# Another order for four pairs of w2 rows in a state-space and dense layer

## The chip, the cores and the metric

The kernel runs on one core of one Trainium2 chip. The metric is device time in microseconds (us). The engines are TensorE (PE, with its weight loads as PEld), VectorE (DVE), ScalarE (ACT), GpSimd (POOL) and SyncE (SP), which here only issues transfers. SP, ACT and POOL each have a queue of transfers; all queues share the core's 16 DMA engines.

## The reference

The input x is 2048 tokens by 1024. After a layer norm (xn) the output is the sum of x, a diagonal complex state-space layer and a dense layer, in bfloat16:

```python
xn = _layernorm(x, axis=-1)
return x + _A_ref(xn, A_Lambda_re, ..., A_Dskip) + _B_ref(xn, B_w1, B_b1, B_w2)

# A: Bu = xn @ B_bar^T (complex); h_t = Lam_bar * h_(t-1) + Bu_t
#    y = 2 * real(h @ C^T) + xn * Dskip
# B: h = xn @ w1 + b1 (1024 -> 3584);  act = h * tanh(softplus(h))
#    act @ w2 (3584 -> 1024)
```

The activation is Mish. "Dense 1" below is xn @ w1, "dense 2" is act @ w2.

## The kernel before, in words

**Blocks.** The tokens are worked in four blocks of 512. Each block runs dense 1 with Mish, the input product of the state-space layer (B), a rotation, a scan along the tokens, the rotation back, and then dense 2 and the output projection (C), which add up in the same eight PSUM banks; DVE adds x and empties the banks (L1676), and the rows go out. The first block does all this plainly. The second does dense 2 plainly, but most of dense 1 and the B product by a scheme with seven products of halves in place of eight; the third and fourth use such a scheme for dense 2 too.

**Order.** The order of the work is written out by hand: one string of short names for each block (FIRST, WHOLE, STEPS, LAST), walked by `perform`. Each operation goes to its engine's list with the waits that its tiles call for; an engine works its list strictly in order. So a wait of an instruction holds all that stand behind it on that engine, and a transfer leaves when its queue's engine comes to it.

**The ring.** Weights stream through seven slots of 4 KB per partition (`ring`). SP issues one load each time that PE, and where told ACT, has done with a slot. The list `items` fixes what is loaded; for the first two blocks the dense 2 part of it is

```python
items += [("w2", g) for g in W2_ORDER]
```

A pair g is two tiles of 128 w2 rows, 2g and 2g + 1, of 28. `in_order(n, us)` runs tile 2 * W2_ORDER[n // 2] + n % 2 for the PSUM banks us, and the strings name n alone (`da20` is the n-th tile in order, not tile 20). A pair is 16 matmuls with 512 columns (L1544), whose stationary operand is a piece of the tile of `act` with the same number. `row_sizes` (first block) and `sizes_of` with `late_sizes` (second block, for the last four pairs) have ACT take the absolute row sums of the w2 rows in the slot (L1312, L1319) and follow the same table.

**What waits for act tiles.** When dense 2 has read an act tile, its memory takes something else. In the second block `m2` has POOL load raw w2 rows in two halves, the first into act tiles 20 to 23 and the second into tiles 24 to 27 (`d2_load`, L1264); `m3` loads two more halves into tiles 8 to 15. `h8` to `h11` scale the rows on ACT (L1279), POOL stores some of them to the DRAM buffer w2d (L1269), and four steps on DVE (`kd0`, L1297) turn them into the sums that the third block's dense 2 needs; each overwrites a half that must have been stored. Both halves of one load count on one semaphore. In the first block POOL loads rows of the B matrices into act tiles (`rows_load`, L1443), of which the fifth waits for tile 21 by an extra line; ACT takes their sizes (L1448).

**Around the end of the second block.** SP issues four DMA transposes of the next block's xn (`tr0` to `tr3`, L653) between the ring loads of C (`ring<-ctd`). PE's first products of the third block (L1063) write banks that DVE has to empty first, and some read units that DVE makes in place (L1238).

Of the kernel before, what the change touches and what calls it, by code (L numbers as in the profile page):

```python
# [142 lines left out]
def bass_parallel_sum__ssm_conv_s5__dense_activation_mish__prompt_kernel(  # L143
    nc: bass.Bass,
    A_x: bass.AP,
    A_Lambda_re: bass.AP,
    A_Lambda_im: bass.AP,
    A_B_re: bass.AP,
    A_B_im: bass.AP,
    A_C_re: bass.AP,  # L150
    A_C_im: bass.AP,
    A_log_dt: bass.AP,
    A_Dskip: bass.AP,
    B_x: bass.AP,
    B_w1: bass.AP,
    B_b1: bass.AP,
    B_w2: bass.AP,
    out: bass.AP,
):
    build_kernel(nc, A_x, A_Lambda_re, A_Lambda_im, A_B_re, A_B_im, A_C_re, A_C_im,  # L160
                 A_log_dt, A_Dskip, B_w1, B_b1, B_w2, out)


def build_kernel(nc, A_x, A_Lambda_re, A_Lambda_im, A_B_re, A_B_im, A_C_re, A_C_im,
# [19 lines left out]
    GROUPS = ((0, 7), (7, NPL), (NPL, NPL + 8), (NPL + 8, NF), (12, 16), (16, 20), (20, 24), (24, 28))  # L184
    TILES = [*range(12)]
    NFG = {2: 5, 3: GF}
    W2_ORDER = tuple(range(14))
    EARLY, LATE = ((0, 20),), ((20, 28),)
    PLAIN = [(f, f + 1) for f in (24, 10, 12, 26)]
    PASSING = {}  # L190
# [252 lines left out]
    for blk in range(NB):  # L443
# [7 lines left out]
        else:  # L451
            items += [("w2", g) for g in W2_ORDER]
        items += [("c", j) for j in range(NJ)] if blk >= FAST else []
# [853 lines left out]
    def row_sizes(g):  # L1307
        s = (NF // 2 + g) % NRING
        for j in range(2):
            r = 2 * W2_ORDER[g] + j  # L1310
            src = ring[:, s, j * D:(j + 1) * D]
# [3 lines left out]
    def late_sizes(g, s):  # L1315
        for j in range(2):
            r = 2 * W2_ORDER[g] + j
            src = ring[:, s, j * D:(j + 1) * D].rearrange("p (d t) -> p d t", d=2)
            aop(lambda e, src=src, r=r: e.activation(CT[:, 0:2, 1, TB:D], src, AF.Abs, accum_out=wp[:, r:r + 1]),  # L1319
                reads=[b_ring[s]], writes=[b_snap[0], b_wp])  # L1320
# [207 lines left out]
    def perform(blk):  # L1528
# [10 lines left out]
        for f0 in range(20, NF, 2) if blk == FAST else ():  # L1539
            left[at_item[blk, "w2", W2_ORDER[f0 // 2]]] += 1  # L1540

# [32 lines left out]
        def dense(f, us, chained=False):  # L1574
            g = (4 * REAL[f // 4] + f % 4) // 2 if split else f // 2
            at = at_item[blk, "w2", g]
            s = at % NRING
            assert n_item[0] <= at < n_loaded[0]
            wt = ring[:, s, :].rearrange("p (f d) -> p f d", f=2)
            for u in us:  # L1580
                q, h = u // 2, u % 2
                t, b_t = place(blk, f)
                opens = first[u]
                first[u] = False
                mm2(u, t[:, q * P:(q + 1) * P], wt[:, f % 2, h * TB:(h + 1) * TB], [b_t, b_ring[s]], at, opens=opens,
                    chained=chained, tell=f % 2 == 1 and u == us[-1])

        def in_order(n, us):
            dense(2 * W2_ORDER[n // 2] + n % 2, us)

        def sizes_of(g):
            at = at_item[blk, "w2", W2_ORDER[g]]
            late_sizes(g, at % NRING)
            if used(at):
                release()
# [279 lines left out]
```

## Time and profile before

| | |
|---|---|
| median of 3 runs | 591.37 us (590.75 to 593.43) |
| profiled execution, its own time | 591.81 us |
| its span | 590.6 us |
| PE busy in the span | 582.7 us |
| DVE, ACT, POOL busy | 511.2, 402.0, 151.9 us |
| first block's dense 2 on PE (L1544, act) | from 85.07, 48.51 us |
| second block's dense 2 on PE | from 228.97, with its last 218 matmuls from 232.01 |
| second block's output projection on PE | from 279.06, 27.79 us |
| transferred | 160.84 MB, mean 272 GB/s |

A row of a timeline gives start and length in us, engine, line and operation, output and inputs, and in brackets how long the engine was idle before and what ended that. DMA issues are counted from the issuing instruction to the landing of the data. The granted clock was 1.0 throughout.

### The profile page before, as it was taken

Reading aid. Unit: us, or ns where it says so; the run is one execution under the profiler, and the core shown is the slowest. Engines: PE = TensorE matmul, PEld = TensorE weight load, DVE = VectorE, ACT = ScalarE, POOL = GpSimd, SP = SyncE. Lnnn points to the kernel's source line nnn. Section 1 sums busy time; section 2 is a strip of 40 time slices with the busy share of each in tenths; the row PEclk is TensorE's granted clock in tenths of the full one; section 3 lists DMA queues with packets and bytes.
Section 4 is the critical chain, followed back from the end, with each engine's and each line's share of the span. In section 5 each row is a group of like instructions: output and inputs, shape, how many; then the busy total and the mean of one; then the engine's idle time right before and its main releaser. Section 6 shows DMA issues by size and latency. Waiting matters only on the chain.

```text
span 590.6 us, 9767 instructions
## 1 busy us (share of the span) xinstructions
PE 582.7 (99%) x3631; PEld 353.0 (60%) x3631; DVE 511.2 (87%) x784; ACT 402.0 (68%) x541; POOL 151.9 (26%) x215
## 2 busy tenths in 40 slices
PE   9999999999999999999999999999999999999998
PEld 8644444444447887444448888644446888854444
DVE  6999999999796878998957789999997569789995
ACT  4859995489297778999636779976222788892330
POOL 2899200134424421332161243200000013100000
DMA  9999999999668987999999959998945946989832
GB/s 242 309 243 263 231 179 221 316 326 361 226 243 279 322 291 262 338 309 207 273 396 394 348 205 299 333 335 252 290 157 196 388 184 214 339 320 317 296 118 72
DMA packets 115369, 160.84 MB, mean 272 GB/s; under 512 B 55802, under 2 KB 66682, under 8 KB 115322
## 3 DMA queue, kind: packets, MB, share of 16 engines
q1 hardware_dynamic: 98512, 107.31, 60.6%
q0 software_dynamic: 13728, 45.62, 22.4%
q10 hardware_dynamic: 3082, 7.29, 3.4%
q8 instruction: 29, 0.48, 0.3%
q14 instruction: 18, 0.15, 0.1%
HBM read 114.05 MB, written 34.08 MB: 251 GB/s over the span
## 4 chain that ended last, share of the span: by engine, by line
PE 88%; DMA 5%; DVE 3%; ACT 3%; issue 1%; POOL 0%; DVEq 0%
PE ps L1544 44%; PE ps L1063 15%; PE ps L985 11%; PE ps L1755 10%; PE ps L1773 5%; DMA act<-in_B_w_dram 2%; DMA w2d<-act 1%; PE ps L713 1%; DMA ring<-w2d 1%; PE ps L722 1%; DMA w2d<-hb 1%; DVE xx L1676 1%; ACT act L1279 1%; ACT hb L1279 1%; PE ps L675 1%
## 5 line engine op out<-in xcount | busy, mean ns | idle before, releaser
L1544 PE MATMUL ps<-ring,act 128*128 128x512 bf16 (+1 forms) x716 | 156.2, 379 | 0.0
L1544 PEld LDWEIGHTS ps<-ring,act 128*128 128x128 bf16 (+1 forms) x716 | 70.0, 98 | 83.3 <-DMA ring<-w2d 0.2
L1544 PE MATMUL ps<-ring,hT 128*128 128x512 bf16 (+1 forms) x390 | 83.4, 376 | 0.0
L1083 ACT ACTIVATE snaps<-ps,par,cs 128x256 f32<-128x256 f32 x100 | 54.5, 562 | 40.8 <-PE ps L1063 38.5
L947 DVE TENSOR_TENSOR mt<-hT,tab 128x2048 bf16<-128x2048 bf16 (+1 forms) x56 | 68.0, 1214 | 0.4
L1544 PEld LDWEIGHTS ps<-ring,hT 128*128 128x128 bf16 x390 | 38.1, 98 | 45.0
L1406 DVE TENSOR_TENSOR_SCAN hT<-cs,qi,hT 128x512 bf16<-128x512 f32 x48 | 60.1, 1273 | 0.0
L1063 PE MATMUL ps<-TT,ring 128*128 128x256 f16 x480 | 59.8, 273 | 0.0
L1755 PE MATMUL ps<-xnT,ring 128*128 128x512 bf16 x264 | 57.3, 379 | 0.0
L1100 DVE SCALAR_TENSOR_TENSOR act<-ps,cs,snaps 128x512 bf16<-128x512 f32 x54 | 39.4, 747 | 16.0 <-PE ps L1063 13.9
L1063 PE MATMUL ps<-xnT,ring 128*128 128x256 bf16 x400 | 50.4, 273 | 1.4 <-DVE xx L1676 1.4
L1063 PEld LDWEIGHTS ps<-TT,ring 128*128 128x128 f16 (+1 forms) x480 | 46.8, 98 | 6.5
L1269 POOL DMA_DIRECT2D w2d<-hb x35 | 25.0, 716 | 87.4 <-ACT hb L1279 50.4
L1755 PEld LDWEIGHTS ps<-xnT,ring 128*128 128x128 bf16 x264 | 25.8, 98 | 31.0
L1063 PEld LDWEIGHTS ps<-xnT,ring 128*128 128x128 bf16 (+1 forms) x400 | 38.9, 98 | 6.8 <-issue 1.9
L1650 ACT ACTIVATE hT<-hT,wz 128x1024 bf16<-128x1024 bf16 x16 | 18.0, 1146 | 36.5 <-DVE hT L1646 36.5
L931 ACT ACTIVATE act<-act 128x2048 bf16<-128x2048 bf16 (+3 forms) x13 | 33.0, 2559 | 2.0 <-DVE act L1086 1.9
L1010 DVE TENSOR_TENSOR hT<-ps,snaps 128x512 f16<-128x512 f32 x36 | 23.8, 687 | 11.9 <-ACT snaps L1002 10.0
L938 ACT ACTIVATE act<-act,cs 128x512 bf16<-128x512 bf16 x48 | 30.8, 708 | 0.1
L1212 POOL DMA_DIRECT2D wsd<-hb x35 | 19.0, 546 | 42.2 <-DVE hb L1238 25.4
L1766 ACT ACTIVATE act<-ps,par 128x512 bf16<-128x512 f32 (+1 forms) x40 | 23.6, 660 | 8.2 <-PE ps L1755 8.2
L1223 ACT ACTIVATE hb<-hb,cs 128x2048 bf16<-128x2048 bf16 x10 | 19.4, 1995 | 14.1 <-DVE xx L1676 12.7
(237 smaller groups left out, 1038.2 us busy)
## 6 DMA issues: line engine op xcount, KB each, us to landing
ring<-wsd SPq DMA_DIRECT2D x110, 256.0 KB, 4.9
ring<-in_B_w_dram SPq DMA_DIRECT2D x52, 512.0 KB, 5.5
ring<-ctd SPq DMA_DIRECT2D x24, 512.0 KB, 4.6
ring<-w2d SPq DMA_DIRECT2D x24, 512.0 KB, 4.7
ring<-w2d SPq DMA_DIRECT2D x36, 256.0 KB, 4.6
wsd<-hb POOLq DMA_DIRECT2D x35, 256.0 KB, 4.8
w2d<-hb POOLq DMA_DIRECT2D x35, 256.0 KB, 5.1
hb<-in_B_w_dram POOLq DMA_DIRECT2D x20, 256.0 KB, 5.4
```

Source lines behind the costliest of these rows:

```text
L931: aop(lambda e: e.activation(t, t, AF.Mish), reads=b, writes=b)
L938: aop(lambda e, a=a, y=y: e.activation(a, a, AF.Copy, scale=y), reads=[b_a, b_y], writes=[b_a])
L947: vop(lambda e: e.tensor_tensor(mt[:], u.unsqueeze(1).to_broadcast([P, 2, 2, TB]), tab[:, :, j, :].unsqueeze(2).to_broadcast([P, 2, 2, TB] ...
L985: PE.mm(lambda e, w=w, x=x, o=o, begin=begin, end=end: e.matmul(ps[:, bank, o:o + TH], lhsT=w, rhs=x, start=opens and begin, stop=end, ski ...
L1063: PE.mm(lambda e, w=w, x=x, o=o, begin=begin, end=end: e.matmul(ps[:, bank, o:o + TH], lhsT=w, rhs=x, start=opens and begin, stop=end, ski ...
L1083: aop(lambda e, o=o, p=p, j=j: e.activation(o, p, AF.Identity, scale=ig, bias=b1(f0 + j)), reads=[b_ps[b], b_par, b_ig], writes=b_dst)
L1100: vop(lambda e: e.scalar_tensor_tensor(out=dst, in0=bank(b), scalar=ig, in1=src, op0=ALU.mult, op1=ALU.add), reads=[b_ps[b], b_snap[k], b_ ...
L1269: PO.dma(lambda e: e.dma_start(w2d[at // 4][:, at % 4 * TB:(at % 4 + 2) * TB].rearrange("p (j t) -> p j t", j=2), t[:, :, d, :]), sem, rea ...
L1406: vop(lambda e: e.tensor_tensor_scan(out=hT[:, ci, j, :], data0=cj("r", j).to_broadcast([P, TB]), data1=hT[:, ci, j, :], initial=init, op0 ...
L1544: PE.mm(lambda e: e.matmul(ps[:, bank, lo:hi], lhsT=lhsT, rhs=rhs, start=opens, stop=last, skip_group_check=split), reads=reads, writes=[b ...
L1755: PE.mm(lambda e, k=k, w=w: e.matmul(ps[:, bank, :], lhsT=w, rhs=xnT[:, k, :], start=k == 0, stop=k == NK - 1), reads=[b_ring[s]] + b_xnT, ...
L1773: PE.mm(lambda e, ci=ci, k=k: e.matmul(ps[:, bank + ci, :], lhsT=BT[:, ci, j, k, :], rhs=xnT[:, k, :], start=k == 0, stop=k == NK - 1), re ...
```

## The change

One table is given another order:

```diff
-    W2_ORDER = tuple(range(14))
+    W2_ORDER = (*range(10), 12, 10, 11, 13)
```

Dense 2's last four pairs are loaded and multiplied in the order 12, 10, 11, 13, so the act tiles are read in the order 24, 25, 20, 21, 22, 23, 26, 27. The numbers of instructions and transfers are the same. The table serves the first and the second block; the third and fourth don't use it.

On PE, this is the second block's dense 2 near its end: a row with x15 ends a place (one pair of w2 rows); the names in brackets are what the matmul ahead of it waits for (d_ring1 to d_ring3: ring loads; q_ac: ACT). The changed row opens the last place but one; the row behind it belongs to the same place.

```order
 L1544 MATMUL ps<-ring,act 128x512 [waits d_ring1]
 L1544 MATMUL ps<-ring,act 128x512 x15
-L1544 MATMUL ps<-ring,act 128x512 [waits d_ring2,q_ac]
+L1544 MATMUL ps<-ring,act 128x512 [waits d_ring2]
 L1544 MATMUL ps<-ring,act 128x512 x15
 L1544 MATMUL ps<-ring,act 128x512 [waits d_ring3]
```

Tile 24, the first of the last group of four to get its Mish from ACT, was first read at the last place but one; now it is read two places earlier, where PE waits for ACT anyway, and its former place, which holds tiles 22 and 23 now, waits for the ring alone.

On POOL, this is the list around the second block's raw w2 loads; it reads the same in both kernels (q_pe: PE; L1212 stores units of w1, L1269 stores scaled w2 rows).

```order
L1212 DMA wsd<-act 128x1024 [waits q_ac]
L1212 DMA wsd<-act 128x1024
L1212 DMA wsd<-act 128x1024 [waits q_ac]
L1264 DMA act<-in_B_w_dram 128x2x1024 [waits q_pe] x2
L1264 DMA act<-in_B_w_dram 128x2x1024 x2
L1269 DMA w2d<-act 128x2x512 [waits q_ac] x2
L1269 DMA w2d<-act 128x2x512
```

The first of the two waiting loads needs tiles 20 to 23. The last matmul that reads them has moved from the third-last place to the last but one; the other load still needs tiles 26 and 27, read at the last place.

The third piece is POOL at the end of the first block, where w1 units are loaded into act tiles 24 to 27 and then 20 to 23 (L1137), behind the carry of the scan (L1419, L1421):

```order
 L1419 TENSOR_TENSOR qi<-qi,qt 128x8 [waits q_po]
 L1421 TENSOR_TENSOR qi<-qi,qt 128x8 [waits q_po]
-L1137 DMA act<-in_B_w1_dram 128x4x256 [waits q_pe] x2
+L1137 DMA act<-in_B_w1_dram 128x4x256
+L1137 DMA act<-in_B_w1_dram 128x4x256 [waits q_pe]
 L1137 DMA act<-in_B_w1_dram 128x4x256
 L1137 DMA act<-in_B_w1_dram 128x4x256 [waits d_nat4]
```

The load into tiles 24 and 25 no longer has a wait for PE of its own, since POOL waited for a later matmul before (tile 21, for L1443).

## The prediction

> **What bounds the kernel now.** I read the page's busy times first, then PE's own waits, then the chain of waits around the second block's end.
>
> ```profile
> PE 582.7 (99%) x3631; PEld 353.0 (60%) x3631; DVE 511.2 (87%) x784; ACT 402.0 (68%) x541; POOL 151.9 (26%) x215
> PE ps L1063 <- DVE xx L1676: 1.4, 1, 1.4
> PE ps L1063 <- DVE act L1238: 1.3, 1, 1.3
> ```
>
> TensorE (PE) is busy for 582.7 of 590.6 us, and no matmul goes away. What a new order can win lies in PE's waits (the columns are total us, times, longest). These two make 2.70 us together. The next rows, PE's timeline, place them at the seam between the second block's projection and the third block's first products.
>
> ```profile
> 232.01 47.22 PE L1544 MATMUL ps<-ring,act 128*128 128x512 bf16 x218
> 279.06 27.79 PE L1544 MATMUL ps<-ring,hT 128*128 128x512 bf16 x128
> 308.29 1.03 PE L1063 MATMUL ps<-xnT,ring 128*128 128x256 bf16 x8 [1.43 <-DVE xx L1676]
> 314.08 1.05 PE L1063 MATMUL ps<-TT,act 128*128 128x256 f16 x8 [1.27 <-DVE act L1238]
> ```
>
> The chain of waits (start, us, what) says why DVE is late there:
>
> ```profile
> 279.65 11.96 DMA act<-in_B_w_dram
> ...
> 291.63 4.28 ACT act L1279 x4
> ...
> 297.07 6.91 DMA w2d<-act
> ...
> 304.06 0.70 DVE act L1297
> ...
> 307.01 4.53 DVE xx L1676 x4
> ...
> 313.43 0.61 DVE act L1238
> ```
>
> Raw w2 rows come from DRAM into act tiles 20 to 27 in two halves. The half issued at 279.65 takes 11.96 us; only then can ACT scale the rows (L1279), POOL store them, and DVE overwrite them (L1297). DVE runs in order, so its L1676, which empties PSUM for PE, and its L1238 are late as well. From 304.06 to 314.04 DVE has no idle time worth naming, so this stretch moves as one piece.
>
> **What the change moves.** I count the pairs of dense 2 as places 0 to 13. From 232.01 to 279.06 PE runs 218 matmuls, 0.2158 us each; a place has 16, so 3.45 us. Place 13 starts at 275.6, place 12 at 272.15.
>
> ```profile
> 272.62 0.72 POOL L1264 DMA_DIRECT2D act<-in_B_w_dram  x1 [1.93 <-PE ps L1544]
> 279.65 2.14 POOL L1264 DMA_DIRECT2D act<-in_B_w_dram  x3 [6.32 <-PE ps L1544]
> ```
>
> The first half writes tiles 20 to 23. Before, their last reader stood at place 11 and the load followed at 272.62. With 12, 10, 11, 13 it stands at place 12, so the load is issued at 272.62 + 3.45 = 276.07. The second half needs tiles 26 and 27, still at place 13, and stays at 279.65 with the two loads behind it. On POOL nothing but these waits behind the moved load. ACT waits for both halves by one semaphore, so the 3.45 us cost nothing directly as long as the first half lands before the second: by its row below it landed at 283.1, the second at 291.6.
>
> What changes is the traffic that it meets. These rows, the DMA issues in narrow windows (one issue each; last number: us from issue to landing), are in order of issue, at 262.49, 265.92, 272.55, 272.62, 274.95 and 279.65:
>
> ```profile
> xnT<-xn SPq DMA_TRANSPOSE x1, 5.1
> xnT<-xn SPq DMA_TRANSPOSE x1, 4.3
> xnT<-xn SPq DMA_TRANSPOSE x1, 10.2
> act<-in_B_w_dram POOLq DMA_DIRECT2D x1, 512.0 KB, 10.5
> xnT<-xn SPq DMA_TRANSPOSE x1, 14.0
> act<-in_B_w_dram POOLq DMA_DIRECT2D x1, 512.0 KB, 12.0
> ```
>
> Between them SP issues loads of the C rows; one in the earlier, quieter stretch, at 262.05, and the two transposes at the raw loads read:
>
> ```profile
> ring<-ctd SPq DMA_DIRECT2D x1, 512.0 KB, 4.4
> 272.55 1.24 SPq L653 DMA_TRANSPOSE xnT<-xn  x1
> 274.95 1.59 SPq L653 DMA_TRANSPOSE xnT<-xn  x1
> ```
>
> Four equal transposes: the first two took 5.1 and 4.3 us, the third, issued 0.07 us before the first half, 10.2, and the fourth, into which the second half runs, 14.0. The table by stretches (last columns: DMA share, GB/s) shows what such a meeting does to all transfers:
>
> ```profile
> 268.00:270.00 2.00, 2.00 (x12) 0.88 (x10) 2.00 (x4) 2.00 (x2) 1.11 (x2) 1.00 1.14 293
> 276.00:278.00 2.00, 2.00 (x11) 0.89 (x10) 1.39 (x9) 1.91 (x4) 0.00 (x0) 1.00 1.09 114
> 286.00:288.00 2.00, 2.00 (x11) 0.94 (x10) 1.93 (x4) 0.91 (x1) 0.00 (x0) 1.00 0.27 77
> 288.00:290.00 2.00, 2.00 (x11) 0.89 (x10) 1.90 (x3) 0.00 (x0) 0.00 (x0) 1.00 1.03 393
> ```
>
> While a raw load and a transpose are in flight together the rate falls to 114 and 77 GB/s; alone, or after, it is 293 to 393. Now there are two such meetings, one after the other. With the first half issued at 276.07 the third transpose, at the 4.3 to 5.1 us of its predecessors, ends at 276.9 to 277.7, when the load has barely begun. One meeting, with the fourth, is left.
>
> How much earlier the second half lands (call it d) the trace of before doesn't show, so I bound it. From the good side: ACT's next free moment. From the bad side: the second half queues behind the first in POOL's queue and is pushed by the whole 3.45 us.
>
> ```profile
> 279.24 7.66 ACT L1223 ACTIVATE hb<-hb,cs 128x2048 bf16<-128x2048 bf16 x4
> 291.63 4.27 ACT L1279 ACTIVATE act<-act,cs 128x1024 bf16<-128x1024 bf16 x4 [4.72 <-DMA act<-in_B_w_dram]
> ```
>
> ACT idles 4.72 us, so d lies between -3.45 and 4.72. Between: if the first half meets the fourth transpose as it met the third, it lands at 276.07 + 10.5 = 286.6; the second half's 512 KB behind it, at half of 393 GB/s because SP's ring loads share the engines, take 2.7 us more: 289.3, so d = 2.3. If there is no real meeting any more, d reaches 4.72. I take 2.3 to 4.7, nearer the low end.
>
> PE gains as much as d until its own waits are gone: the projection ends at 306.85, and the 2.70 us are all there is. Below that DVE isn't the limit either: the last L1676 (4.53 / 4 = 1.13 us) can start at 306.85, which with the 2.5 us from its end (311.54) to that of L1238 (314.04) gives 310.5, before PE is there at 314.08 - 2.70 = 311.38. So the term is -2.3 to -2.7; I take -2.4.
>
> [...]
>
> **The other moved parts.** The new place 10 needs tile 24 earlier. ACT's last Mish of this block ends at 241.79, PE comes to place 10 at 265.2; no cost, with 23 us of cover.
>
> ```profile
> 234.49 7.30 ACT L931 ACTIVATE act<-act 128x2048 bf16<-128x2048 bf16 x4
> ```
>
> The table W2_ORDER also serves the first block, which the few words on the change don't say. There the loads of projection rows (L1443) wait for tile 21, which is now read a place later:
>
> ```profile
> 124.13 0.54 POOL L1443 DMA_DIRECT2D act<-in_A_B_re_dram  x1 [11.97 <-PE ps L1544]
> 131.04 1.06 ACT L1448 ACTIVATE act<-act 128x1024 bf16<-128x1024 bf16 x1 [0.23 <-DMA act<-in_A_B_re_dram]
> 135.90 1.28 DVE L866 SCALAR_TENSOR_TENSOR CT<-CT,cs,ct 128x1024 bf16<-128x1024 bf16 x1
> 158.66 2.36 DVE L1676 TENSOR_TENSOR xx<-ps,xx 128x1024 bf16<-128x1024 f32 x2 [3.15 <-PE ps L1544]
> ```
>
> So 124.13 becomes 127.58. ACT already waits 0.23 us for the third of these loads at 131.04; it will wait about 3.4 us more, and the scaling that DVE needs for its L866 at 135.90 shifts from an end near 133.2 to 136.6. I estimate 0.7 us of delay on DVE. It has 3.15 us of idle time before 158.66, so PE sees nothing; without that cover it would cost 0.7 us. POOL's later loads and ACT's scalings shift by up to 3.5 us, before ACT's long idle time. Ring loads are as many and as large as before; which w2 rows they fetch costs nothing.
>
> **The sum.** The profiled execution took 591.81 us (its span of 590.57 and 1.24 around it): 591.81 - 2.4 = 589.4. It lies 0.44 us above the median of 591.37, so the median becomes 589.0.
>
> **Rivals.**
>
> First, no change, 591.4 (590.9 to 591.9). The second half meets the fourth transpose whatever the first does, and it is the one on the chain. For it: its issue at 279.65 doesn't move, and the low rates last until 288. Against: it landed in a queue that had just spent 10 us on the first half and third transpose, which also held up the fourth.
>
> [...]
>
> Third, slower: the first half, now 3.45 us closer to the second, meets the fourth transpose and both loads pile up on it. From the moment that the second half lands after 291.61 every us costs PE one us, since DVE is full from 304 to 314. At the whole 3.45 us: 594.8; at half, 593.1. For it: POOL's queue holds the two in order, and the fourth transpose is the slowest already. Against: the third transpose and a ring load leave the engines earlier, and the data of both halves are no more than before.
>
> Fourth, the first block decides: the row loads slip by more than 3.45 us in the traffic of their time, and DVE's delay exceeds 3.15 us; each us above costs one. At a slip twice as large, with DVE delayed by 4.2 us, it takes back 1.0 us: with the gain 590.0, without it 592.4.
>
> **How the numbers follow.** Forecast 0.58, first and second rival together 0.22, the third 0.14, the fourth 0.06. The forecast's own range is 588.2 to 590.2: the 2.70 us and a few tenths of a median's scatter below, half of the gain above. For 8 in 10 I go over the unchanged case to 592.2, the weaker part of the third rival's. The bound of 0.5% (about what a measurement of this kernel can tell from no change) is 2.96 us. The two waits hold 2.70, so faster by over that needs the whole of them and some help from scatter or from later stretches: a third of the forecast, 0.20. Slower by over 0.5% needs 594.3, most of the pile-up and a little of the fourth: 0.11. The rest, 0.69, is within 0.5%.
>
> **What would show it.** The first half issued at about 276.1 (the step on the places); the third transpose landing in about 5 us instead of 10.2 (the meeting); the second half landing at 287 to 289.5 and ACT's L1279 starting then; DVE's L1297 starting before 302; PE's waits at the seam below 0.5 us together. It is wrong if the third transpose is fast and the second half lands no earlier, if DVE's L1676 starts at 307 or later, or if the idle time before 158.66 in the first block is gone.

## The result, and the profile after

| | before, same chip | changed |
|---|---|---|
| median of 11 executions | 593.25 us (590.29 to 596.26) | 588.03 us (587.57 to 591.76) |
| profiled execution, its own time | 591.81 us | 587.96 us |
| its span | 590.6 us | 586.7 us |

The ratio is 0.9927, with a 95% interval of 0.9901 to 0.9953: the changed kernel is 0.5 to 1.0% faster on this chip. The forecast was 589.0, with a range of its own from 588.2 to 590.2; 588.03 lies 0.17 us below that range, and the gain of 0.73% is nearly double the 0.4% forecast. The before column holds a second lesson: its eleven executions spread over 6 us, ten of the eleven changed ones over 0.75 us (587.57 to 588.32).

PE's waits of the changed kernel (total us, times, longest), the three largest:

```profile
PE ps L675 <- DVE filler L499: 1.0, 1, 1.0
PE ps L713 <- DMA ring<-in_B_w_dram: 0.7, 2, 0.5
PE ps L1544 <- DMA ring<-w2d: 0.7, 2, 0.5
```

Both waits of L1063, 1.4 and 1.3 us before, are gone. POOL's timeline and the DMA issues show where that comes from. The issues (KB, and last the us from issue to landing) stand in order of issue: four transposes at 262.78, 266.21, 272.84 and 275.24, then the raw halves at 276.37 and 279.94.

```profile
276.37 0.72 POOL L1264 DMA_DIRECT2D act<-in_B_w_dram  x1 [5.39 <-PE ps L1544]
279.94 2.14 POOL L1264 DMA_DIRECT2D act<-in_B_w_dram  x3 [2.86 <-PE ps L1544]
```

```profile
xnT<-xn SPq DMA_TRANSPOSE x1, 5.5
xnT<-xn SPq DMA_TRANSPOSE x1, 4.4
xnT<-xn SPq DMA_TRANSPOSE x1, 4.6
xnT<-xn SPq DMA_TRANSPOSE x1, 5.8
act<-in_B_w_dram POOLq DMA_DIRECT2D x1, 512.0 KB, 7.8
act<-in_B_w_dram POOLq DMA_DIRECT2D x1, 512.0 KB, 7.2
```

The whole execution runs 0.30 us later up to here (the projection starts at 279.36, before at 279.06). Less that, the first half leaves at 276.07, where the prediction had put it, and the second has not moved. The last two transposes take 4.6 and 5.8 us in place of 10.2 and 14.0, the second half 7.2 in place of 12.0. The table by stretches has the rates (last column, GB/s), 278 and 393 where 114 and 77 stood; over the eight stretches from 272 to 288 us the mean is 291 in place of 154:

```profile
276.00:278.00 2.00, 2.00 (x11) 0.88 (x10) 1.73 (x10) 1.88 (x4) 0.72 (x1) 1.00 1.06 278
286.00:288.00 2.00, 2.00 (x11) 0.89 (x10) 1.93 (x4) 2.00 (x2) 0.00 (x0) 1.00 1.03 393
```

The rest of the chain, in the timelines of ACT, DVE and PE:

```profile
287.16 8.51 ACT L1279 ACTIVATE act<-act,cs 128x1024 bf16<-128x1024 bf16 x8
```

```profile
297.85 2.94 DVE L1297 TENSOR_TENSOR act<-act 128x1024 f16<-128x1024 bf16 x4 [0.58 <-DMA w2d<-act]
302.00 1.22 DVE L1676 TENSOR_TENSOR xx<-ps,xx 128x1024 bf16<-128x1024 f32 x1 [1.22 <-PE ps L1544]
```

```profile
279.36 27.79 PE L1544 MATMUL ps<-ring,hT 128*128 128x512 bf16 x128
306.98 1.04 PE L1063 MATMUL ps<-xnT,ring 128*128 128x256 bf16 x8
311.35 1.04 PE L1063 MATMUL ps<-TT,act 128*128 128x256 f16 x8
```

ACT starts on the raw rows 4.47 us earlier and straight behind its work before (L1223 ends at 287.2). DVE's L1297 starts at 297.85 where it started at 304.06, and the releaser at L1676 has changed sides: DVE now waits for PE.

**What it brought.** From the projection's start to the row of TT PE took 314.08 - 279.06 = 35.02 us before and 311.35 - 279.36 = 31.99 after: 3.03 us. The two waits account for 2.70. The rest is overlap: without a wait the first L1063 starts 0.17 us ahead of the projection's end at 307.15 and the row of TT 0.16 us ahead of the end of the row before it at 311.51, and such a start was lost at each of the two waits (0.33 us together).

The other part of the 3.85 us between the two spans (590.57 and 586.72) lies elsewhere, in the third block's dense 2, where PE waits for weights. Before:

```profile
383.04 1.04 PE L1544 MATMUL ps<-ring,S 128*128 128x512 f16 x4 [1.06 <-DMA ring<-w2d]
384.94 3.19 PE L1544 MATMUL ps<-ring,S 128*128 128x512 f16 x14 [0.87 <-DMA ring<-w2d]
```

After:

```profile
380.57 3.20 PE L1544 MATMUL ps<-ring,S 128*128 128x512 f16 x14 [0.47 <-DMA ring<-w2d]
385.85 14.42 PE L1544 MATMUL ps<-ring,act 128*128 128x512 bf16 x66 [0.18 <-DMA ring<-w2d]
```

That is 1.93 us of waiting against 0.65. Over the profiled executions below, with the change and without, this wait scatters from 0.3 to 1.6 us, so I don't count it to the change. 3.03 + 1.28 - 0.30 (the later start) = 4.01, within 0.16 of the difference.

### The profile page after: what moved, and what is told of

Its sections match the earlier page's. It is cut to its first block, busy times and chain, and to the rows that moved or that the text cites. A ratio compares the mean times of both kernels' runs of the same rounds, so it can differ in the third digit from the quotient of the medians.

```text
span 586.7 us, 9766 instructions
## 1 busy us (share of the span) xinstructions
PE 581.6 (99%) x3631; PEld 351.4 (60%) x3631; DVE 512.3 (87%) x784; ACT 401.9 (68%) x541; POOL 151.8 (26%) x215
## 4 chain that ended last, share of the span: by engine, by line
PE 96%; DMA 2%; SPq 1%; issue 0%; DVE 0%
PE ps L1544 49%; PE ps L1063 19%; PE ps L985 13%; PE ps L1755 10%; PE ps L1773 5%; DMA ring<-in_B_w_dram 1%; PE ps L722 1%; DMA ring<-w2d 1%; PE ps L713 0%; SPq L428 0%; SPq L481 0%; PE ps L547 0%; SPq L489 0%; SPq L432 0%; DVE xx L1709 0%
## 5 line engine op out<-in xcount | busy, mean ns | idle before, releaser
L1063 PE MATMUL ps<-TT,ring 128*128 128x256 f16 x480 | 59.8, 273 | 0.0
L1063 PEld LDWEIGHTS ps<-TT,ring 128*128 128x128 f16 (+1 forms) x480 | 46.8, 98 | 6.5
L1063 PE MATMUL ps<-xnT,ring 128*128 128x256 bf16 x400 | 50.4, 273 | 0.0
L1269 POOL DMA_DIRECT2D w2d<-hb x35 | 25.0, 716 | 87.6 <-ACT hb L1279 50.6
L1063 PEld LDWEIGHTS ps<-xnT,ring 128*128 128x128 bf16 (+1 forms) x400 | 39.0, 98 | 5.2
L1212 POOL DMA_DIRECT2D wsd<-hb x35 | 19.0, 546 | 43.8 <-DVE hb L1238 33.5
L1773 PE MATMUL ps<-xnT,BT 128*128 128x512 bf16 x128 | 27.8, 379 | 0.0
```

What stands on the lines that cost most here:

```text
L1063: PE.mm(lambda e, w=w, x=x, o=o, begin=begin, end=end: e.matmul(ps[:, bank, o:o + TH], lhsT=w, rhs=x, start=opens and begin, stop=end, ski ...
L1269: PO.dma(lambda e: e.dma_start(w2d[at // 4][:, at % 4 * TB:(at % 4 + 2) * TB].rearrange("p (j t) -> p j t", j=2), t[:, :, d, :]), sem, rea ...
L1773: PE.mm(lambda e, ci=ci, k=k: e.matmul(ps[:, bank + ci, :], lhsT=BT[:, ci, j, k, :], rhs=xnT[:, k, :], start=k == 0, stop=k == NK - 1), re ...
```

## The experiments

The theory: a raw w2 load on POOL's queue beside DMA transposes on SP's holds up both, and this makes the second half late. Rivals are that the first block did it, that the order as such did it, or that the transfers' volume did it. Each label is one kernel with 12 executions on one chip, where the kernel before was run as well. Line numbers are those of before, except in the two kernels with extra transfers, where they are five higher from L1269 on.

The outcome needed another count than a median. On these chips most times of before lie between 587.1 and 589.7 us (the low level below) and a part above 590 (the high level), with a handful between. I therefore count executions above 590 us; the bound was set after seeing the first results, and with 589.5 or 590.5 the last table comes out alike. Executions whose granted clock shows 0.997 or less (21 in all) lie above 590 whichever the kernel; they are left out of this count.

**One block at a time.** The table becomes one for each block:

```diff
-    W2_ORDER = tuple(range(14))
+    W2_ORDERS = (tuple(range(14)), (*range(10), 12, 10, 11, 13))
```

with `W2_ORDERS[blk]` where it is used. This one has the new order in the second block alone:

> New order 12, 10, 11, 13 in the second block alone; the first block keeps 10, 11, 12, 13. Theory (the meetings of raw w2 loads and transposes): everything won comes from here. Third and fourth transposes land in 4 to 6 us, ACT's L1279 starts straight after its L1223, PE has no wait at the seam; the time is that of the changed kernel, 588.0, or up to 0.6 us less, and DVE's idle time before the first block's L1676 is back near 3 us. Rival (the first block's new order has a part in it): less than three quarters of the 4 to 5 us are won.

Measured: 588.27 us (587.21 to 589.48), none of 12 above 590, ratio 0.9982 (0.9960 to 1.0003). Its profile has no wait of PE at the seam. DVE's idle time before the first block's L1676 is back, but at 1.38 us and not near 3; it is 1.43 in the second profile of before, further down. And with the two entries exchanged:

> New order in the first block alone. Theory: no gain; the row loads of the first block start 3.5 us later and DVE's L866 waits about 3 us for ACT, within the 3 us of idle time before L1676, so the time is that of the kernel before within 0.3%. The two waits of PE at the seam stay at 2 to 4 us. Rival (the first block has a part in the gain): at least 1.2 us faster than before.

Measured: 588.54 (587.76 to 591.72), 2 of 12 above 590, ratio 0.9993 (0.9969 to 1.0016). Its profiled execution is one at the low level (587.76): PE has no wait at the seam, where 2 to 4 us were expected, although the third and fourth transposes take 9.1 and 8.9 us; the second half lands after 7.6. Before beside them: 588.30 (587.29 to 593.40), 7 of 32. The gain expected as a fixed 4 to 5 us is not there on this chip, because before itself is at the low level in most executions; about 1 us is won in the mean, less than the three quarters by which the rival would be known, but the first block's order alone wins nothing that can be told from none. What the second block's order seems to take away is the high level; for one kernel that is weak evidence (at a share of 7 in 32, twelve executions without one come about in about one case of twenty by chance), and the counts of all kernels at the end carry it.

**The transposes moved in place of the load.** The order of the pairs is the old one; the third and fourth transpose go right behind the second, in the string of the second block:

```diff
-             "da19 tr1 n2 ... ls10 tr2 da22 da23 ls11 tr3 da24 ...
+             "da19 tr1 tr2 tr3 n2 ... ls10 da22 da23 ls11 da24 ...
```

> Old order everywhere, raw loads where they were (272.6 and 279.7); the third and fourth transposes are issued right behind the second, at about 267 to 269, so that both raw loads find no transpose. Theory (the meetings): the gain of the change without the change, PE's waits at the seam under 0.5 us, ACT's L1279 at about 287, time 587.5 to 589. A remaining risk is that the early transposes meet the stores at 268 to 270; these have 3 us before the first raw load. Rival (what counts is that the first load leaves POOL later, or the order of the w2 rows): no gain, 590.5 to 593.

Measured: 588.42 (587.45 to 588.82), none of 12 above 590, ratio 0.9978 (0.9958 to 0.9999). Its profile, the transposes on SP's queue and the scaling on ACT:

```profile
266.16 5.59 SPq L653 DMA_TRANSPOSE xnT<-xn  x3
```

```profile
287.10 8.41 ACT L1279 ACTIVATE act<-act,cs 128x1024 bf16<-128x1024 bf16 x8
```

The raw half still leaves at 272.9 and the pairs stand in the old order, yet ACT starts at 287.10. With the counts below, the order of the pairs is only one way to the same end. The expectation that both raw loads would find no transpose failed: the fourth leaves at 269.8 and takes 7.2 us, so it overlaps the raw half for 4.1 us.

**The new order, with the meeting put back.** The order of the first kernel above, and the two transposes one ring load later:

```diff
-             "... ls10 tr2 da22 da23 ls11 tr3 da24 da25 ls12 da26 ...
+             "... ls10 da22 da23 ls11 tr2 da24 da25 ls12 tr3 da26 ...
```

> New order in the second block (as e1), but the third and fourth transposes are issued one ring load later, at about 275 and 277.5, into the raw load of 276.4 and the one of 279.9. Theory (the meetings): they are back; the two transposes take 8 us or more, the second half lands at 290 or later, PE waits 2 us or more at the seam, time 590 to 594. Rival (the load's later place is enough by itself): it stays at 588.

Measured: 588.80 (587.40 to 593.64), 3 of 10 above 590, ratio 1.0010 (0.9984 to 1.0037). The raw half leaves at 275.68, the transposes 1.1 us ahead and 1.3 us behind it:

```profile
274.60 1.23 SPq L653 DMA_TRANSPOSE xnT<-xn  x1
277.00 1.23 SPq L653 DMA_TRANSPOSE xnT<-xn  x1
```

The high level is back with the new order of pairs. That most executions would lie there was wrong: about a third do. The profiled one, at 587.40, isn't among them (its transposes take 4.3 and 6.6 us, and PE doesn't wait at the seam), so that the seam makes the high level of this kernel is not shown by a trace.

**The two kernels again, on another chip.**

> The changed kernel beside the kernel before on one chip, where the times of the latter spread from 587 to 593 (10 of 35 above 590 in the first study). Theory (a meeting of raw load and transpose goes wrong in some executions only, and the change takes the meeting away): the lower end of both kernels is the same within 0.5 us, at most 1 of 12 of these lies above 590, and the medians differ by less than 0.3% where few of before's go wrong. Rival (the change saves a fixed time): all its times lie 2 us or more below those of before.

Measured: 588.41 (587.53 to 589.40), none of 12 above 590, ratio 0.9971 (0.9945 to 0.9997).

> The kernel before, for one more profile. Theory: where its profiled time is near 588, its third and fourth transposes land in 4 to 9 us and PE's waits at the seam are under 0.5 us, with all issues where they were; where it is above 590, the transposes take 10 us or more and PE waits 2.5 us or more there. Rival: the seam looks alike in both, and the spread comes from another place.

Measured: 588.86 (587.20 to 595.28), 3 of 11 above 590; before beside it 588.77 (587.14 to 594.32), 9 of 33. The profiled execution of before is one at the low level (588.72), and so shows what the first profile of before could not:

```profile
272.96 0.72 POOL L1264 DMA_DIRECT2D act<-in_B_w_dram  x1 [1.93 <-PE ps L1544]
```

```profile
xnT<-xn SPq DMA_TRANSPOSE x1, 7.4
xnT<-xn SPq DMA_TRANSPOSE x1, 6.7
act<-in_B_w_dram POOLq DMA_DIRECT2D x1, 512.0 KB, 6.4
```

```profile
287.16 8.41 ACT L1279 ACTIVATE act<-act,cs 128x1024 bf16<-128x1024 bf16 x8
```

(third and fourth transpose, second raw half.) All is issued 0.34 us later than in the first profile, the fourth transpose 0.86. The third transpose is only mildly slowed, the fourth less, and ACT isn't late at all. The cost thus differs from execution to execution of one kernel.

**Volume, or meeting.** The old order with two extra 512 KB transfers on POOL's queue behind the first raw half, of w2 rows into a DRAM buffer that nobody reads:

```diff
+            for i in range(2 if g == 2 and h == 0 else 0):
+                queue.dma(lambda e, i=i, src=src: e.dma_start(scr[i].rearrange("p (j d) -> p j d", j=2), src),
+                          DmaSem(nc, "d_scr%d" % i), writes=[Buf("scr%d" % i)])
```

> Old order, and POOL issues two more transfers of 512 KB (the same w2 rows into a DRAM buffer that nobody reads) right behind the first raw load, so that its queue is full during the third and fourth transposes. Theory (the meetings): they go wrong in most executions; most times above 590, median 591 to 595. Volume alone: the second half lands up to 2.7 us later, which costs PE under 1 us (588 to 589).

Measured: 589.46 (587.71 to 595.36), 3 of 10 above 590, ratio 1.0003 (0.9969 to 1.0038). The profiled execution (593.16) is at the high level. PE's waits, the DMA issues (third and fourth transpose, second half) and ACT:

```profile
PE ps L1063 <- DVE xx L1681: 3.3, 1, 3.3
PE ps L1063 <- DVE act L1238: 1.3, 1, 1.3
```

```profile
xnT<-xn SPq DMA_TRANSPOSE x1, 9.0
xnT<-xn SPq DMA_TRANSPOSE x1, 18.1
act<-in_B_w_dram POOLq DMA_DIRECT2D x1, 512.0 KB, 15.0
```

```profile
294.34 4.26 ACT L1284 ACTIVATE act<-act,cs 128x1024 bf16<-128x1024 bf16 x4 [7.76 <-DMA act<-in_B_w_dram]
```

The same extra transfers with the transposes moved ahead as above:

> The same two extra transfers, with the third and fourth transposes issued early, behind the second (at 267 to 269). Same volume, no transpose to meet. Theory (the meetings): 588 to 589.5, at most 2 of 12 above 590. Rival (the volume on POOL's queue is what delays the second half): as slow as the run with the longer meeting, within 0.5 us.

Measured: 588.31 (587.50 to 589.16), none of 12 above 590, ratio 0.9962 (0.9937 to 0.9987).

```profile
287.21 4.27 ACT L1284 ACTIVATE act<-act,cs 128x1024 bf16<-128x1024 bf16 x4 [0.48 <-DMA act<-in_B_w_dram]
```

The volume is equal in these two, so volume isn't it. Nor is it a meeting as such: against the expectation, here the third transpose is in flight from about 267.8 to 275.7 us and the fourth from 270.7 to 277.3, while the raw half leaves at 272.33 and takes 7.3 us, so both overlap it. What this kernel lacks is a transpose issued behind the raw half. But a longer meeting didn't bring the high level about more often than the plain one (3 of 10 against 3 of 11), as it should have by the expectation; in the one profile it made it dearer, 4.6 us of waits in place of 2.7.

**Both halves late.** The old order, but POOL issues the second half first and the first behind it:

```diff
-        for h in range(2):
+        for h in ((1, 0) if g == 2 else range(2)):
```

> Old order; only the two halves change places on POOL: the second half first (it waits for place 13, so it leaves at about 279.7) and the first right behind it at 280.4. No load leaves at 272.6. Theory (the meetings): both transposes have the engines to themselves until 280, no meeting, at most 1 of 12 times above 590, median within 0.5 us of the changed kernel, although this load leaves 4 us later than in the changed kernel. Rival (pile-up: the halves behind each other land too late, after 291): most times above 590.

Measured: 588.09 (587.55 to 594.98), none of 11 above 590, ratio 0.9968 (0.9936 to 1.0000).

```profile
279.47 2.85 POOL L1264 DMA_DIRECT2D act<-in_B_w_dram  x4 [8.84 <-PE ps L1544]
```

```profile
286.76 8.41 ACT L1279 ACTIVATE act<-act,cs 128x1024 bf16<-128x1024 bf16 x8
```

Both halves leave together and ACT still has them in time. So how close the halves stand costs nothing here, and how much earlier the first leaves is worth nothing. (Its fourth transpose, issued at 274.99, takes 5.7 us and is still in flight for 1.2 us of the halves.)

**The changed kernel on this third chip, and another order.**

> The changed kernel once more, for the share of disturbed times beside those of the kernel before in this call. Theory: at most 1 of 12 above 590, whatever share of before's lies there; the ratio of the two goes with that share (about 1% where all lie there, 0.3% where a third does). Rival (a fixed gain): the same ratio everywhere.

Measured: 588.17 (587.47 to 591.08), none of 11 above 590, ratio 0.9975 (0.9945 to 1.0006). And with the other two pairs exchanged, in the second block alone, so that the first half's tiles are read where they were:

```diff
+    W2_ORDERS = (tuple(range(14)), (*range(12), 13, 12))
```

> Another new order in the second block, 10, 11, 13, 12, which leaves both raw loads where they were before (272.6 and 279.7). Theory (the meetings): as the kernel before, with a share of times above 590 like its own. Rival (the order of the products or of the w2 rows in DRAM matters by itself): like the changed kernel, none above 590.

Measured: 588.85 (588.10 to 593.28), 3 of 10 above 590, ratio 0.9991 (0.9957 to 1.0024); before beside these: 589.82 (587.38 to 595.01), 8 of 25. Its profiled execution (590.93), the longer of PE's two waits at the seam, the third and fourth transpose with the second half, and ACT:

```profile
PE ps L1063 <- DVE xx L1676: 2.0, 1, 2.0
```

```profile
xnT<-xn SPq DMA_TRANSPOSE x1, 10.5
xnT<-xn SPq DMA_TRANSPOSE x1, 13.8
act<-in_B_w_dram POOLq DMA_DIRECT2D x1, 512.0 KB, 12.7
```

```profile
292.49 4.27 ACT L1279 ACTIVATE act<-act,cs 128x1024 bf16<-128x1024 bf16 x4 [5.46 <-DMA act<-in_B_w_dram]
```

Another order of the pairs with the old issue time leaves the high level where it was.

**Overlap, or a transpose behind the load.** In the changed kernel the fourth transpose (275.24 to 281.0) and the first half (276.37 to 284.2) overlap for 4.7 us without harm, as they do for 4.1 and 5.0 us in the two kernels with early transposes. So overlap may not be what hurts. Kernels with the high level have a transpose that is issued once the raw load is under way; those without have none. The old order, with one transpose left at the load's side and none behind it:

```diff
-             "da19 tr1 n2 ... ls10 tr2 da22 da23 ls11 tr3 da24 ...
+             "da19 tr1 tr2 n2 ... ls10 tr3 da22 da23 ls11 da24 ...
```

> Old order of the pairs; the third transpose goes right behind the second (about 267), and the fourth takes the third's former place, some 0.07 us ahead of the first raw half (issued about 272.6, as before). So one transpose overlaps the raw load over nearly its whole length, and none is issued once the raw load is under way. Overlap theory (a transpose in flight together with a raw load is enough): executions above 590 stay about as often as with the old order on this chip, 24 of 90 so far, so 2 to 5 of 12, and in the profile the last transpose lands after 7 us or more. Behind theory (only a transpose that is issued while the raw load is under way gets stuck; the changed kernel, where the fourth transpose leaves 1.1 us ahead of the load and both overlap for 4.7 us without harm, and the kernel with late transposes, where it leaves 0.6 us behind the load, would fit it): no execution above 590 at the full clock, median 588.2 to 588.5, last transpose under 7 us.

(The 0.6 us it gives for the kernel with late transposes should read 1.3, as shown above.) Measured: 588.26 (587.59 to 589.24), none of 12 above 590, ratio 0.9968 (0.9950 to 0.9987); before beside it, on a fourth chip, 590.60 (587.75 to 592.53), 8 of 15. SP's queue, POOL, and the issues from 272.3 to 272.7:

```profile
272.52 2.31 SPq L653 DMA_TRANSPOSE xnT<-xn  x1
```

```profile
272.59 0.72 POOL L1264 DMA_DIRECT2D act<-in_B_w_dram  x1 [1.93 <-PE ps L1544]
```

```profile
act<-in_B_w_dram POOLq DMA_DIRECT2D x1, 512.0 KB, 6.2
xnT<-xn SPq DMA_TRANSPOSE x1, 7.3
```

The transpose beside the load takes 7.3 us, which by the letter of the expectation was a sign of the overlap theory; the count, which is what costs time, goes against it. It is mild slowing as in the low profile of before. What went away with the transpose behind the load is the high level. This kernel also has one transpose fewer beside the raw half than before; that the number alone isn't what counts is shown by the kernel with extra transfers and early transposes, where two overlap the half and none of 12 lies above 590.

**All counts together**, executions at the full clock above 590 us:

| | above 590 | highest |
|---|---|---|
| no transpose issued behind the raw load (changed kernel on three chips, second block alone, early transposes, with and without extra transfers, both halves late, none behind) | 0 of 92 | 589.48 |
| a transpose behind it: first block alone, late transposes, longer meeting, other pairs, and before again | 14 of 53 | 595.36 |
| a transpose behind it: before beside them, on four chips | 32 of 105 | 593.22 |

## Why the prediction was right or wrong

**Right: the place, and the chain from the second half to PE's waits.** The first half's issue was met to 0.01 us, the second's didn't move, the third transpose took 4.6 us (forecast about 5), L1279 started at 287.16 (287 to 289.5), L1297 at 297.85 (before 302), and PE's waits at the seam are gone. The early transposes give the gain without the change, the late ones take it from the change. Why the third transpose and both halves were slow was right only in part (next point).

**Wrong: "one meeting, with the fourth, is left", and d nearer its low end.** That step sized d at 2.3 to 4.7 and leaned to 2.3, letting the first half meet the fourth transpose at the price of the old meeting, 10.5 us. It took 7.8, and the second half behind it landed at 287.1, so that d reached its upper bound, ACT's idle time. The step took overlap for the cause. The last experiment, the two kernels with early transposes and the changed profile show overlap costing a few us of a transfer at most (the transposes beside a raw half took 5.8 to 7.9 us) and PE nothing; a transpose that enters behind a raw load under way is what all kernels with the high level share. The rates by which the prediction told a meeting were read too narrowly as well: the changed kernel has 109 GB/s from 272 to 274 us, before any raw load has left.

**Wrong: a cap of 2.70 for PE.** The waits' own times left out the overlap of neighbouring matmuls that each of them cost (0.17 and 0.16 us in the changed profile); the seam brought 3.03. With the 1.28 us of chance in the third block, the profiled execution reached 587.96 in place of 589.4.

**Wrong: one profile as the price.** The sum took 2.4 us from every execution. The runs show an event that comes in 22 to 53% of the executions of before on four chips (7 of 32, 9 of 33, 8 of 25, 8 of 15). By the times alone it came in all 11 of the first comparison, none of which was under 590.29; their clock is not on record, save for the profiled execution's 1.0. The change takes the event away and leaves the other executions as they were: on the two chips where both were run again, the executions of before below 590 average 588.40 and 588.51 us, the changed kernel's at the full clock 588.33 and 588.27. So its worth is what the event cost on average: 0.73% in the first comparison, 0.25 to 0.3% on the two chips after it. That 589.0 came as near as it did was thus in part luck: the base of 591.37 and the profile both came from where before was always high, and the gain of 0.4% would have been above what the two later chips showed. That also explains the chance of 0.20 for faster by over 0.5%: it hung on the whole of two fixed waits and on scatter, and I hadn't seen that before's scatter, 590.75 to 593.43 in three executions, was itself the thing removed.

**The first rival (no change)** fell with the second half's 7.2 us; as a description of an execution at the low level it is right, since there before has nothing to win. **The second** shares the chance of 0.22 with the first; no run shows what it assumed, and its part of the chance was an estimate of the author's. What the runs show: in the changed kernel the last three transposes each land about 1 us behind the ring load of twice the size that SP issued just ahead (the transposes take 4.4, 4.6 and 5.8 us, the loads 3.8, 4.0 and 5.2). In the first profile of before the third and fourth take 10.2 and 14.0 us, the loads ahead of them 4.4 and 9.9, and over the three profiles at the high level these transposes take 9.0 to 18.1. **The third (pile-up)** failed in the result, where the second half took 7.2 us, and once more with both halves issued together at 279.47 and 588.09 us.

**The fourth (first block)** came closer than its chance of 0.06 said. What DVE's L866 waits for is ACT's L865, before and after; ACT itself waits for the moved load, whose issue stands below it (KB, us to landing). Before:

```profile
133.14 1.13 ACT L865 ACTIVATE ct<-CT,cs 128x1024 f32<-128x1024 bf16 x1
```

```profile
act<-in_A_B_re_dram POOLq DMA_DIRECT2D x1, 256.0 KB, 4.1
```

After, and DVE's rows:

```profile
133.96 1.06 ACT L1448 ACTIVATE act<-act 128x1024 bf16<-128x1024 bf16 x1 [4.94 <-DMA act<-in_A_B_re_dram]
...
138.14 1.13 ACT L865 ACTIVATE ct<-CT,cs 128x1024 f32<-128x1024 bf16 x1
```

```profile
127.88 0.54 POOL L1443 DMA_DIRECT2D act<-in_A_B_re_dram  x1 [15.42 <-PE ps L1544]
```

```profile
act<-in_A_B_re_dram POOLq DMA_DIRECT2D x1, 256.0 KB, 6.1
```

```profile
139.30 1.28 DVE L866 SCALAR_TENSOR_TENSOR CT<-CT,cs,ct 128x1024 bf16<-128x1024 bf16 x1 [3.03 <-ACT ct L865]
159.54 4.61 DVE L1676 TENSOR_TENSOR xx<-ps,xx 128x1024 bf16<-128x1024 f32 x4
```

The load left at 127.58 + 0.30 as forecast, but L866 came 3.1 us late (139.30 - 135.90 - 0.30), not 0.7. Two terms failed. I had taken the scaling that L866 needs to end near 133.2, which is the end of L864; L865, the one that it waits for, ended at 134.27, so 1.1 us of the supposed slack was not there. And the load took 6.1 us in place of 4.1, so ACT slipped by 138.14 - 133.14 - 0.30 = 4.7 us and not by 3.4. The cover of 3.15 us is used up, and L1676 starts 0.58 us late. By the prediction's own words this sign counts against it. PE still shows no wait there, and the time agrees: with the first block's order alone 588.54, before beside it 588.30. The place has no reserve left.

**Open:** why the first comparison had the event in every execution and the later chips had it in 22 to 53%; what decides it within an execution; and what in the queues is held up. SP's ring loads issued behind the raw half are held up too (9.9 to 13.7 us in the first profile of before; the same loads take 5.2 to 7.2 in the changed kernel), so it isn't the transposes alone. The sign "behind" was read out of the earlier runs and put to the test by one kernel, with 12 executions, so it holds for this kernel's high level and is not a rule.

## What to carry to other kernels

Where DMA transposes on one queue and large loads on another may come together, try issuing the transposes first, so that none follows a load under way; moving the transposes did as well here as moving the load (on one chip 588.42 us and 588.27, none of 12 above 590 in either). Look at the spread of the times and at several executions before pricing a wait from one profile: a wait that comes in some executions only is worth its cost times its frequency, and a change that removes it shows in the highest times before it shows in the median. When a wait on the bottleneck engine goes away, add the overlap at its place to its idle time (0.17 and 0.16 us in this one profile).

## What the runs showed of the hardware

- A 256 KB transpose that takes 4.1 to 6.5 us with no raw load under way took 9.0 to 18.1 in the three profiled executions at the high level (the fourth 13.8 to 18.1), and the second raw half took 12.0 to 15.0 where it takes 7.8 or less in the others. From 272 to 288 us the core moved 154 GB/s in the mean in the first of these, 291 in the changed kernel. Nearly the same issue times in two other executions gave 7.4 and 6.7, and 9.1 and 8.9 us for the transposes without a wait of PE.
- Overlap of a raw half with a transpose issued ahead of it did no harm: for 4.7 us in the changed kernel (5.8 and 7.8 us), 4.1 and 5.0 us in the kernels with early transposes.
- How often it happens differed: 8 of 15, 8 of 25, 9 of 33 and 7 of 32 executions of one and the same kernel on four chips, and 11 of 11, by the times alone, in the first comparison.
- Executions with a granted clock of 0.997 or less were above 590 us in every kernel that had any, the changed one too (591.08 and 591.76). They make 3 of 95 executions without a transpose behind the raw load and 18 of 176 with one; whether the wait at the seam has a part in the lower clock stays open.
